# Weight tiles fetched three ahead at 1.25 a slot, k and q loaded as whole rows, and one output tile moved to another PSUM bank, in a linear-attention and two-MLP kernel

## The chip, the cores and the metric

The kernel runs on one core of a Trainium2 chip. The metric is the device time of one execution in microseconds. All times below are microseconds unless marked ns.

## The reference, cut to what matters

Three stages follow each other. The first is a recurrent attention; the other two are MLPs on its output, each with its own nonlinearity. All data are float32.

```python
batch, n_heads, seq, head_dim = (4, 8, 768, 48)
for t in range(S):                                   # attention
    state = alpha[:, :, t, :, None] * state + np.einsum('bhd,bhe->bhde', k[:, :, t], v[:, :, t])
    y[:, :, t] = np.einsum('bhd,bhde->bhe', q[:, :, t], state)
...
x = transpose(y).reshape(3072, 384)
h = x @ w_in                                         # first MLP, w_in 384 x 2048
P = a[0] + a[1] * h + a[2] * h2 + a[3] * h3
Q = 1.0 + np.abs(b[0]) * np.abs(h) + np.abs(b[1]) * h2
x = (P / (Q + 1e-06)) @ w_out                        # w_out 2048 x 384
h = x @ w_in                                         # second MLP
return (h * np.cos(h)) @ w_out
```

The weights come as float64. The kernel reads them as 64-bit words and turns them into float32 on the chip; for the matmuls every float32 operand of the MLPs is then split in a rounded part and the rest, which gives three matmuls for one.

## The kernel before, in words

**Units and slots.** The sequence is cut into 6 chunks of 128 steps; with 4 batches that makes 24 units (`NU`). A unit handles all 8 heads, as 4 pairs: a pair's two heads lie in partitions 0 to 47 and 64 to 111, and the partitions between are padding. A loop over n writes out the program slot by slot. Slot n holds, for different units at once, the stages of a software pipeline: the PE (TensorE) computes `scores(n)`, then `y_state(n - 1)` and `y_scores(n - 1)`, `transposes(n)` and `update0(n - 1)`; ACT (ScalarE) copies and scales (`k_out`, `mask0`, `guess2`, `update2`, `y_out`); DVE (VectorE) computes the decays (`inverse0`, `inverse1`, `guess1`, `decay`, `update1`); POOL (GpSimd) masks and scales k and q (`mask1`, `scale_q`, `scale_k`). Each engine takes its instructions strictly in the written order, so a wait of one instruction holds back all that stand behind it. The program's lines are the order; there is no scheduler.

**Weight tiles.** The first MLP needs 32 weight tiles (16 of `w_in`, 16 of `w_out`), 384 KB each as 64-bit words. `w_fetch` issues the load of the next tile, into one of four places of `spare` (the second x buffer, not yet in use) or of two `raw` buffers; at most six tiles may be begun and not finished (`steps`). `tick(k, ahead)` runs up to k steps of the oldest tile, as long as more than `ahead` tiles are in `steps`. A tile has three steps: the first scales its high words and copies its exponent bytes (L68 on POOL and L69 on ACT while n < 20; L66 and L69, both on ACT, later), the other two are DVE instructions (L73, L74). Then `w_hi` (ACT, L172) rounds the tile and `w_lo` (POOL, L181) forms the rest. While n < 20 the exponent words lie in a PSUM bank (`words_t`, bank b2); from slot 20 on that bank belongs to the MLP and all operands lie in SBUF.

**Loads.** SP (SyncE) issues nearly all DMAs in written order: per slot the unit's a, kq and v, the store of a finished y (`y_store`), and the weight tiles. kq is k and q of a unit, 128 partitions of 4 KB.

**The overlap with the MLPs.** From slot `LEAD` = 20 on, each slot also holds one `layers` step: `gemm1` (9 matmuls of `w_in`, L469), the nonlinearity of earlier tiles (`rational`: ACT, POOL and DVE), and five steps behind, `gemm2` (9 matmuls of `w_out`, L482). Steps after slot 24 hold the MLPs alone. PSUM has eight banks: b0, b1, b2 for `gemm1` (and before that for y, transposes and exponent words), r0 and r1 (r1 holds `fresh`, a constant tile that `decay` and `last_decay` read up to slot 20), and acc0 to acc2 for `gemm2` (and before that for the scores and for the state update u, which lies in acc2).

Of the kernel before, what the change touches and what calls it, by code (L numbers as in the profile page):

```python
# [16 lines left out]
B, H, S, D = 4, 8, 768, 48  # L17
DM, DFF = 384, 2048
NC, C = 6, 128
HP = 4  # L20
# [3 lines left out]
NU = NC * B  # L24
# [14 lines left out]
def attn_then_two_moe(ctx, tc, kqT, aT, vP, w1i, w1o, ma, mb, w2i, w2o, out):  # L39
# [81 lines left out]
    spare = x_p.tile([128, 2, NK, TB], F32R, tag="x", name="spare").rearrange("p a b c -> p (a b c)").bitcast(I32)  # L121
    raw64 = {}
    stage = {}
    slot = [0]
    fetched = [0, 2 * NF]
    steps = []
    to_hi, to_lo = [], []

    def w_fetch(upto):

        i = fetched[0]
        fetched[1] = upto
        if i >= upto or len(steps) > 5 or sum(j >= 28 for j in range(i - len(steps), i + 1)) > 2:
            return
        w = w_order[i]
        fetched[0] += 1
        if i < 28 and i % 6 < 4:
            flat = spare[:, 2 * DM * (i % 6):2 * DM * (i % 6 + 1)]
        else:
            flat = raw_p.tile([128, 2 * DM], I32, tag="raw", name="raw")  # L140
        nc.sync.dma_start(out=flat, in_=(w1i, w1o, w2i, w2o)[2 * w[0] + w[1]][w[2]].bitcast(I32))
        raw64[w] = flat.rearrange("p (a b) -> p a b", b=2)
        steps.append((w, 0))
# [50 lines left out]

    def load(u, name):

        if u >= NU:
            return
        c, b = divmod(u, B)
        ts = {"a": a_t, "kq": kq_t, "v": v_t}[name]  # L200
        t, src = ts[u % len(ts)], {"a": aT, "kq": kqT, "v": vP}[name][c, b]
        if name == "v":
            nc.sync.dma_start(out=t[:, :H * D], in_=src)
        elif u == 0 and name == "a":
            for cs in (slice(0, HP + HP // 2 * C), slice(HP + HP // 2 * C, HP * (C + 1))):
                nc.sync.dma_start(out=t[:, cs], in_=src[:, cs])
        elif u < len(ts):
            nc.sync.dma_start(out=t, in_=src)
        else:
            for j in range(2):  # L210
                js = slice(64 * j, 64 * j + D)
                nc.sync.dma_start(out=t[js], in_=src[js])
        d = U.setdefault(u, {})
        if name == "kq":
            d["k"], d["q"] = t[:, 0], t[:, 1]
        else:
            d[name] = t
# [128 lines left out]
    def y_state(u):  # L346
        c, b = divmod(u, B)
        d = U[u]
        if u >= NU - B:
            d["y"] = ps_acc.tile([128, HP, C], F32, tag="acc2", name="y")  # L350
        else:
            d["y"] = bank("b1", (128, HP, C))
        if c:
            for hp in range(HP):
                nc.tensor.matmul(
                    d["y"][:, hp, :], s_bd[b][:, hp, :], d["q"][:, hp, :], start=hp == 0, stop=False,
                    skip_group_check=True,
                )
# [19 lines left out]
    def y_store(u):  # L378
        c, b = divmod(u, B)
        rows = xd[0][c].rearrange("(a j e) t -> j e a t", a=HP, j=2)  # L380
        for j in range(2):
            nc.sync.dma_start(out=rows[j][:, :, b * C:(b + 1) * C], in_=U[u]["yo"][64 * j:64 * j + D])

    LEAD = NU - 4

    def attention(n, tick):

        def on(u, more=False):
            return 0 <= u < (NU - B if more else NU)
# [50 lines left out]
            transposes(n)  # L440
        if on(n - 1, True):
            update0(n - 1)
        if on(n - 1):
            y_out(n - 1)
        tick(1 if n < LEAD else 2)
        if on(n) and n >= LEAD:
# [214 lines left out]
    with tc.manual_schedule():  # L661
# [16 lines left out]
        for n in range(-3, NU + 1):  # L678
            slot[0] = n
            if n >= -1:  # L680
                load(n + 4, "a")
            if n >= 0:
                if n:
                    load(n + 2, "kq")
                load(n + 1, "v")
                if n >= 2:
                    y_store(n - 2)
                for i in range(min(n, 1) if n < 4 else 2 - n % 2):
                    w_fetch(2 * NF)
            if n == 3:  # L690
                nc.sync.dma_start(out=cab[:, 0:4], in_=ma.unsqueeze(0).to_broadcast([128, 4]))
                nc.sync.dma_start(out=cab[:, 4:6], in_=mb.unsqueeze(0).to_broadcast([128, 2]))
            if n == 6:
                nc.scalar.activation(out=cq[:, 0:2], in_=cab[:, 4:6], func=AF.Abs)
                nc.vector.tensor_scalar(cq[:, 2:6], cab[:, 0:4], -LN_S * LN_S, None, ALU.mult)
            if 8 <= n < 8 + NK:
                x_load(0, 0, n - 8)
            kk = (n - 12) // 2 if n in (12, 14, 16) else None
            if kk is not None:
                x_hi(0, 0, kk)  # L700
            if n == 1:
                warm_up(8)
            attention(n, lambda k: tick(k, 1 if n < LEAD else 1))
            if kk is not None:
                x_lo(0, 0, kk)
            if n == -3:
                for name, u in (("a", 2), ("kq", 1), ("v", 0), ("kq", 2)):
                    load(u, name)
            w_lo([nc.gpsimd])
            if n >= LEAD:  # L710
                layers(n - LEAD)
        y_store(NU - 1)
        for n in range(NU + 1 - LEAD, 2 * N1 + 4):
            layers(n)
# [171 lines left out]
```

## Time and profile before

| what | value |
|---|---|
| time, median of 3 runs | 1007.4 (1005.34 to 1008.27) |
| the profiled execution: time, and its span | 1006.72, 1005.0 |
| busy in the span: PE, DVE, ACT, POOL | 947.7, 667.5, 661.6, 626.5 |
| mean share of TensorE's full clock granted | 0.961 |

The span runs from the first to the last instruction; the profiled time is 1.7 longer. The profiled execution lies 0.7 below the median. Busy times are sums over stages that differ: about the first 190 are attention, the rest the MLPs.

### The profile page before, as it was taken

To read this page: it belongs to the slowest core of one execution; us is meant where nothing else is said; L and a number is where in the kernel's file an instruction comes from. 1 tells how busy PE (TensorE), PEld (TensorE's weight loads), DVE (VectorE), ACT (ScalarE), POOL (GpSimd) and SP (SyncE) were. 2 spreads that over 40 slices of the span, in tenths; PEclk is the share of its full clock that TensorE was granted. 3 is DMA by queue.
4 is the path that set the end of the run, shared out by engine and by line. 5 is a ranking of instruction groups with operands and counts; after the bars stand their busy time and mean duration, and the time that the engine had idled before them with its cause. 6 is when DMAs were issued, how large, how long until landed. Compare 5 with 4: busy or idle time off the path is not lost. (4 is left out here: it accounts for less than half of the span.)

```text
span 1005.0 us, 14055 instructions
## 1 busy us (share of the span) xinstructions
PE 947.7 (94%) x4824; PEld 762.3 (76%) x4824; DVE 667.5 (66%) x1089; ACT 661.6 (66%) x1210; POOL 626.5 (62%) x585
## 2 busy tenths in 40 slices
PE   6688867999999999999999999999999999999997
PEld 5576655787787788888888887688888888888885
DVE  7787866896999999987878985733434334334331
ACT  4776866886888888877778876644445355444442
POOL 4686876997798999997887865533333333333332
PEclk7877787999999999999999999999999999999999
DMA  6888775400332413202015424110010010200001
GB/s 197 235 227 233 206 207 150 117 1 1 100 121 64 149 41 117 72 1 80 1 63 173 126 85 136 32 63 1 1 64 1 0 63 1 64 1 1 32 0 36
DMA packets 46687, 81.91 MB, mean 82 GB/s; under 512 B 5840, under 2 KB 22480, under 8 KB 46608
## 3 DMA queue, kind: packets, MB, share of 16 engines
q1 hardware_dynamic: 46608, 80.93, 27.0%
q8 instruction: 40, 0.66, 0.3%
q14 instruction: 39, 0.32, 0.1%
HBM read 60.47 MB, written 20.45 MB: 81 GB/s over the span
## 5 line engine op out<-in xcount | busy, mean ns | idle before, releaser
L512 POOL TENSOR_TENSOR lo<-g,hi 128x512 fp32r<-128x512 f32 x192 | 256.1, 1334 | 307.0 <-ACT hi L507 300.2
L469 PE MATMUL b<-x,w 128*128 128x512 f32 x1728 | 436.1, 396 | 6.0 <-DVE g L559 3.2
L482 PE MATMUL acc<-hi,w 128*128 128x512 f32 x1152 | 393.4, 396 | 0.1
L469 PEld LDWEIGHTS b<-x,w 128*128 128x128 f32 x1728 | 323.1, 188 | 89.4 <-DVE g L559 7.2
L482 PEld LDWEIGHTS acc<-hi,w 128*128 128x128 f32 x1152 | 216.2, 188 | 54.4 <-ACT o L500 1.3
L507 ACT ACTIVATE hi<-g 128x512 fp32r<-128x512 f32 x192 | 121.4, 633 | 175.9 <-PE acc L482 114.5
L482 PE MATMUL acc<-lo,w 128*128 128x512 f32 x576 | 227.3, 395 | 0.0
L559 DVE TENSOR_TENSOR g<-ah,b 128x512 f32<-128x512 f32 x96 | 65.6, 684 | 133.0 <-ACT ah L557 133.0
L538 POOL TENSOR_TENSOR z<-z,ah 128x512 f32<-128x512 f32 x96 | 126.0, 1312 | 8.0
L482 PEld LDWEIGHTS acc<-lo,w 128*128 128x128 f32 x576 | 108.1, 188 | 25.8
L80 DVE SCALAR_TENSOR_TENSOR ah<-z,b 128x512 f32<-128x512 int32 x96 | 65.7, 684 | 37.6 <-ACT z L79 37.6
L539 DVE TENSOR_TENSOR g<-g,b 128x512 f32<-128x512 f32 x96 | 65.4, 681 | 37.4 <-ACT g L536 36.8
L79 ACT ACTIVATE z<-b 128x512 int32<-128x512 f32 x96 | 57.2, 596 | 49.8 <-PE b L469 49.8
L537 POOL TENSOR_SCALAR z<-ah,cq 128x512 f32<-128x512 f32 x96 | 75.4, 786 | 6.7 <-ACT ah L535 6.5
L536 ACT ACTIVATE g<-b,cq 128x512 f32<-128x512 f32 x96 | 74.5, 776 | 0.0
L543 DVE SCALAR_TENSOR_TENSOR g<-g,cq,r 128x512 f32<-128x512 f32 x96 | 70.9, 738 | 0.1
L530 DVE SCALAR_TENSOR_TENSOR g<-g,cq,b 128x512 f32<-128x512 f32 x96 | 70.8, 737 | 0.0
L535 ACT ACTIVATE ah<-b 128x512 f32<-128x512 f32 x96 | 56.6, 590 | 20.8 <-PE b L469 20.7
L547 ACT ACTIVATE r<-z,lnb 128x512 f32<-128x512 f32 x96 | 66.7, 695 | 3.7 <-DVE tot L604 3.5
L557 ACT ACTIVATE ah<-ah,half_pi 128x512 f32<-128x512 f32 x96 | 68.2, 711 | 0.0
L532 DVE SCALAR_TENSOR_TENSOR r<-z,r 128x512 f32<-128x512 f32 x96 | 65.7, 684 | 0.0
L527 DVE SCALAR_TENSOR_TENSOR z<-z,r 128x512 f32<-128x512 f32 x96 | 65.2, 679 | 0.0
(94 smaller groups left out, 1040.3 us busy)
## 6 DMA issues: line engine op xcount, KB each, us to landing
kq<-kqT SPq DMA_DIRECT2D x40, 192.0 KB, 4.9
raw<-w2i SPq DMA_DIRECT2D x16, 384.0 KB, 3.1
raw<-w2o SPq DMA_DIRECT2D x16, 384.0 KB, 3.1
w<-wd SPq DMA_DIRECT2D x16, 384.0 KB, 3.2
v<-vP SPq DMA_DIRECT2D x24, 192.0 KB, 3.6
spare<-w1i SPq DMA_DIRECT2D x12, 384.0 KB, 4.1
x<-x0d SPq DMA_DIRECT2D x18, 256.0 KB, 3.3
x1d<-o SPq DMA_DIRECT2D x18, 256.0 KB, 2.3
```

What stands on the lines that cost most here:

```text
L80: nc.vector.scalar_tensor_tensor(r, k, -TWO_PI, h, ALU.mult, ALU.add)
L469: nc.tensor.matmul(h, ws[0][f][:, w, ks], x[:, xx, kk, :], start=i == 0, stop=i == 8)
L482: nc.tensor.matmul(acc[k], ws[1][f][:, w, ks], d[g], start=f == 0 and i == 0, stop=f == NF - 1 and i == 2)
L507: nc.scalar.activation(out=t["hi"], in_=t["g"], func=AF.Copy)
L512: eng.tensor_tensor(out=t["lo"], in0=t["g"], in1=t["hi"].bitcast(F32), op=ALU.subtract)
L530: nc.vector.scalar_tensor_tensor(g, g, cq[:, 3:4], two["h"], ALU.add, ALU.mult)
L536: nc.scalar.activation(out=g, in_=h, func=AF.Identity, scale=cq[:, 5:6], bias=cq[:, 4:5])
L537: nc.gpsimd.tensor_scalar(zz, ah, cq[:, 1:2], cq[:, 0:1], ALU.mult, ALU.add)
L538: nc.gpsimd.tensor_tensor(out=zz, in0=zz, in1=ah, op=ALU.mult)
L543: nc.vector.scalar_tensor_tensor(g, g, cq[:, 2:3], r, ALU.add, ALU.mult)
L547: nc.scalar.activation(out=r, in_=two["z"], func=AF.Ln, scale=LN_S, bias=lnb)
L557: nc.scalar.activation(out=two["r"], in_=two["r"], func=AF.Sin, bias=half_pi)
```

## The change

The change does four things. A tile is converted only when more than three tiles are begun (`tick(k, 3 ...)` in place of 1, for n < 20), and tiles are fetched one a slot and two in each fourth slot, starting at slot 0, in place of one and two in turn from slot 4 on. Since `spare` holds tiles up to number 23 (before: 27) and the two `raw` buffers all later ones, the condition that limits tiles in `raw` is written with the same function. kq is always loaded by one DMA of 128 rows, in place of two of 48 rows. The y of unit 20 goes to bank r1 in place of acc2, and from slot 20 on `y_out` stands behind `layers`.

```diff
+    LEAD = NU - 4
...
+    def in_spare(i):
+        return i < 24 and i % 6 < 4
+
     def w_fetch(upto):
...
-        if i >= upto or len(steps) > 5 or sum(j >= 28 for j in range(i - len(steps), i + 1)) > 2:
+        if i >= upto or len(steps) > 5 or sum(not in_spare(j) for j in range(i - len(steps), i + 1)) > 2:
             return
...
-        if i < 28 and i % 6 < 4:
+        if in_spare(i):
...
-        elif u < len(ts):
+        elif u < len(ts) or name == "kq":
             nc.sync.dma_start(out=t, in_=src)
...
-        if u >= NU - B:
+        if u > LEAD:
             d["y"] = ps_acc.tile([128, HP, C], F32, tag="acc2", name="y")
+        elif u == LEAD:
+            d["y"] = bank("r1", (128, HP, C))
         else:
             d["y"] = bank("b1", (128, HP, C))
...
-        if on(n - 1):
+        if on(n - 1) and n < LEAD:
             y_out(n - 1)
...
-                for i in range(min(n, 1) if n < 4 else 2 - n % 2):
+                for i in range(min(n, 1) if n % 4 else 2):
                     w_fetch(2 * NF)
...
-            attention(n, lambda k: tick(k, 1 if n < LEAD else 1))
+            attention(n, lambda k: tick(k, 3 if n < LEAD else 1))
...
             if n >= LEAD:
                 layers(n - LEAD)
+                y_out(n - 1)
```

**SP, slots 0 to 2** (`spare<-w1i` is a weight tile's load, `kq<-kqT` the load of k and q, `x0d<-g` a store of y). Before:

```order
L203 DMA v_107<-vP 128x384
L212 DMA a_101<-aT 48x516 x2
L208 DMA kq_105<-kqT 128x1024
L203 DMA v_108<-vP 128x384
L141 DMA spare<-w1i 128x768
L212 DMA a_100<-aT 48x516 x2
L212 DMA kq_102<-kqT 48x1024 x2
L203 DMA v_106<-vP 128x384
L382 DMA x0d<-g 48x4x128 x2
L141 DMA spare<-w1i 128x768
```

and with the change:

```order
L208 DMA v_107<-vP 128x384
L145 DMA spare<-w1i 128x768 x2
L217 DMA a_101<-aT 48x516 x2
L213 DMA kq_105<-kqT 128x1024
L208 DMA v_108<-vP 128x384
L145 DMA spare<-w1i 128x768
L217 DMA a_100<-aT 48x516 x2
L213 DMA kq_102<-kqT 128x1024
L208 DMA v_106<-vP 128x384
L389 DMA x0d<-g 48x4x128 x2
L145 DMA spare<-w1i 128x768
```

The first two tiles now stand ahead of slot 1's loads, the third and fourth where the first and second stood, and kq is one row in place of two. In both programs the first conversion step stands in slot 2.

**ACT, slot 21** (`yo` is the copy of unit 20's y, `ah` and the `g` behind it read the first tile of `gemm1`, `sc` is the scores, the `w` rows are `w_hi`). Before:

```order
L66 ACTIVATE st<-raw 128x384
L69 ACTIVATE raw<-raw 128x384
L297 ACTIVATE hi<-sc_1967 128x512
L297 ACTIVATE lo<-sc_1968 128x512
L257 ACTIVATE r_1983<-r_1983 128x512
L258 ACTIVATE r_1983,chk<-r_1983 128x512
L342 ACTIVATE s_bd_144<-s_c_148 48x4x48 x2
L376 ACTIVATE yo<-y 128x512
L535 ACTIVATE ah<-b_1946 128x512
L536 ACTIVATE g<-b_1946,cq 128x512
```

and with the change:

```order
L66 ACTIVATE st<-raw 128x384
L69 ACTIVATE raw<-raw 128x384
L302 ACTIVATE hi<-sc_1906 128x512
L302 ACTIVATE lo<-sc_1907 128x512
L262 ACTIVATE r_1922<-r_1922 128x512
L263 ACTIVATE r_1922,chk<-r_1922 128x512
L347 ACTIVATE s_bd_144<-s_c_148 48x4x48 x2
L540 ACTIVATE ah<-b_1884 128x512
L541 ACTIVATE g<-b_1884,cq 128x512
L176 ACTIVATE w_9_134<-st 128x384
L383 ACTIVATE yo<-r_1939 128x512
```

The copy of y has moved behind the first two instructions of the nonlinearity and reads bank r1.

**DVE, MLP steps 5 and 6** (the first two steps after slot 24; L73 and L74, in the changed file too, are a weight tile's second and third step, the rest the nonlinearity). Before, from the `z` row of step 5 on:

```order
L527 SCALAR_TENSOR_TENSOR z<-z,r_2223 128x512
L530 SCALAR_TENSOR_TENSOR g<-g,cq,b_2152 128x512
L532 SCALAR_TENSOR_TENSOR r_2223<-z,r_2223 128x512
L539 TENSOR_TENSOR g<-g,b_2197 128x512
L543 SCALAR_TENSOR_TENSOR g<-g,cq,r_2223 128x512
L527 SCALAR_TENSOR_TENSOR z<-z,r_2256 128x512
L530 SCALAR_TENSOR_TENSOR g<-g,cq,b_2197 128x512
L532 SCALAR_TENSOR_TENSOR r_2256<-z,r_2256 128x512
```

and with the change:

```order
L532 SCALAR_TENSOR_TENSOR z<-z,r_2162 128x512
L535 SCALAR_TENSOR_TENSOR g<-g,cq,b_2085 128x512
L537 SCALAR_TENSOR_TENSOR r_2162<-z,r_2162 128x512
L544 TENSOR_TENSOR g<-g,b_2136 128x512
L548 SCALAR_TENSOR_TENSOR g<-g,cq,r_2162 128x512
L74 SCALAR_TENSOR_TENSOR st<-raw,st 128x384
L532 SCALAR_TENSOR_TENSOR z<-z,r_2203 128x512
L535 SCALAR_TENSOR_TENSOR g<-g,cq,b_2136 128x512
L537 SCALAR_TENSOR_TENSOR r_2203<-z,r_2203 128x512
L544 TENSOR_TENSOR g<-g,b_2177 128x512
L548 SCALAR_TENSOR_TENSOR g<-g,cq,r_2203 128x512
L73 SCALAR_TENSOR_TENSOR st<-st,raw 128x384
```

Before, all 32 tiles are finished in slot 24; with the change four and a part of a fifth are left for MLP steps 5 to 11. Counted over the whole program, 26 tiles were converted with their exponent words in PSUM and 6 with all operands in SBUF; now 21 and 11. In slots 4 to 19 the L73 rows fall from 24 to 19, and the tiles fetched from 24 to 19.

## Rows read from the trace of the kernel before

**Rows 1.** Windows: each stretch's length, busy us by engine, granted clock, DMA share, GB/s

```profile
34.10:155.70 121.60, 95.82 (x954) 80.59 (x952) 90.89 (x213) 87.35 (x197) 95.21 (x113) 0.78 0.82 219
155.70:180.40 24.70, 17.47 (x158) 14.20 (x155) 14.14 (x27) 15.75 (x35) 16.01 (x16) 0.86 0.47 130
...
195.70:1005.00 809.30, 798.13 (x3405) 637.14 (x3403) 523.02 (x769) 526.76 (x913) 481.27 (x408) 1.00 0.16 53
...
195.70:250.00 54.30, 54.30 (x234) 43.75 (x233) 44.82 (x74) 42.99 (x73) 47.71 (x43) 1.00 0.04 15
```

**Rows 2.** Groups by line, 34.1 to 155.7: busy, mean ns, idle before, releasers

```profile
L181 POOL TENSOR_TENSOR w<-st,w 128x384 fp32r<-128x384 f32 x23 | 24.1, 1058 | 0.0
...
L73 DVE SCALAR_TENSOR_TENSOR b<-st,b 128x384 int32<-128x384 int32 x24 | 13.5, 562 | 22.3 <-POOL st L68 18.3 <-ACT b L69 3.9
...
L74 DVE SCALAR_TENSOR_TENSOR st<-spare,b 128x384 int32<-128x384 int32 x16 | 8.7, 545 | 0.0
L68 POOL TENSOR_SCALAR st<-spare 128x384 f32<-128x384 f32 x16 | 8.5, 533 | 26.2 <-DMA spare<-w1i 19.3 <-DMA spare<-w1o 6.9
...
L69 ACT ACTIVATE b<-spare 128x384 int32<-128x384 uint8 x16 | 8.3, 519 | 29.3 <-DMA spare<-w1i 16.7 <-DMA spare<-w1o 6.5 <-DVE st L74 5.9
```

**Rows 3.** Timeline of ACT, slots 12 to 14: start, us, instruction, idle before

```profile
100.55 0.58 ACT L297 ACTIVATE hi<-sc 128x512 f32<-128x512 f32 x1
...
105.96 0.58 ACT L297 ACTIVATE hi<-sc 128x512 f32<-128x512 f32 x1
...
115.41 0.51 ACT L69 ACTIVATE b<-spare 128x384 int32<-128x384 uint8 x1 [3.55 <-DMA spare<-w1i]
115.86 0.58 ACT L297 ACTIVATE hi<-sc 128x512 f32<-128x512 f32 x1
```

**Rows 4.** Timeline of PE: start of slot 4, then slots 13 and 14

```profile
34.06 1.16 PE L290 MATMUL sc<-kq 48*128 48x128 f32 x16
...
104.12 2.08 PE L355 MATMUL b<-kq,s_bd 128*128 128x128 f32 x8 [1.30 <-ACT g L376]
...
110.10 1.26 PE L290 MATMUL sc<-kq 48*128 48x128 f32 x16
111.29 1.16 PE L355 MATMUL b<-kq,s_bd 128*128 128x128 f32 x8
...
114.08 0.67 PE L322 MATMUL u<-v,g 128*64 128x48 f32 x16
```

**Rows 5.** Timeline, slots 20 to 22, PE and ACT

```profile
155.72 1.16 PE L290 MATMUL sc<-kq 48*128 48x128 f32 x16
...
161.43 0.55 ACT L66 ACTIVATE st<-spare 128x384 f32<-128x384 f32 x1 [3.23 <-DMA spare<-w1o]
...
170.78 2.04 PE L355 MATMUL y<-kq,s_bd 128*128 128x128 f32 x8 [6.19 <-DVE s_c L336]
...
174.66 2.60 PE L469 MATMUL b<-x,w 128*128 128x512 f32 x9
...
180.40 2.36 PE L469 MATMUL b<-x,w 128*128 128x512 f32 x9
```

**Rows 6.** DMA, 34.1 to 155.7: GB/s in 40 slices; issues, KB, us to landing

```profile
GB/s 172 276 327 181 215 156 194 322 277 258 190 227 242 184 289 192 344 219 109 249 221 266 217 144 235 160 246 236 122 269 188 281 202 133 247 228 301 145 74 235
...
kq<-kqT SPq DMA_DIRECT2D x34, 192.0 KB, 4.9
spare<-w1i SPq DMA_DIRECT2D x9, 384.0 KB, 3.9
```

**Rows 7.** The page's DMA issues: the first units' kq, whole rows

```profile
kq<-kqT SPq DMA_DIRECT2D x4, 512.0 KB, 4.1
```

**Rows 8.** Groups by line, 300 to 400: weight steps with all operands in SBUF

```profile
L74 DVE SCALAR_TENSOR_TENSOR st<-raw,st 128x384 int32<-128x384 int32 x10 | 12.6, 1264 | 0.1
...
L73 DVE SCALAR_TENSOR_TENSOR st<-st,raw 128x384 int32<-128x384 int32 x10 | 7.8, 783 | 0.4 <-ACT raw L69 0.2
```

**Rows 9.** Timeline of PE at MLP step 5

```profile
193.53 2.37 PE L469 MATMUL b<-x,w 128*128 128x512 f32 x9 [1.07 <-DVE g L530]
```

More of the change, by code (lines that the diff above doesn't have):

```diff
@@ L382, in y_store @@
             nc.sync.dma_start(out=rows[j][:, :, b * C:(b + 1) * C], in_=U[u]["yo"][64 * j:64 * j + D])
-    LEAD = NU - 4
     def attention(n, tick):
```

## Prediction

> **What bounds the kernel now.** I first cut the span into stages, by windows [rows 1]. From 195.7 to the end, 809.3, PE is busy 798.1 at the full granted clock: a step of 18 large matmuls takes 809.3 / 192 = 4.2, and nothing but fewer PE waits can shorten this part. So the kernel's time is the moment at which PE becomes saturated, plus about 809. What the change touches lies ahead of that. In the stretch 34.1 to 155.7, slots 4 to 19 (121.6, or 7.6 a slot), no engine is saturated: PE 95.8, POOL 95.2, DVE 90.9, ACT 87.4 busy.
>
> Why they idle there is shown by the groups by line [rows 2]. The weight tile's first step waits for its load: POOL sat idle 26.2 ahead of L68, ACT 23.2 (16.7 + 6.5) ahead of L69, both until a DMA landed, and DVE 18.3 ahead of L73 for POOL. These are the same waits seen from three engines, not a sum. The timeline of ACT shows the pattern [rows 3]: from the score copy of slot 12 to that of slot 13 is 105.96 - 100.55 = 5.4, and to the next 9.9, of which 3.55 is ACT standing before L69 for a tile that was issued in the same slot. Everything behind it in ACT's order, the score copies first, is held too.
>
> The second place is slots 20 and 21 [rows 5]. From the scores of unit 20 (155.72) to the third MLP tile (180.40) go 24.7, in which PE is busy 17.5 [rows 1]. PE waits 6.19 at the first matmul of unit 20's y, because that y shares bank acc2 with the state update, and in the slot before ACT waits 3.23 for a weight tile.
>
> **The change part by part.**
>
> *Tiles three ahead, 1.25 a slot (slots 4 to 19).* A tile loaded two slots before its use has some 12 us to land; loads take 3.9 [rows 6]. I take the DMA waits of L68 and L69 as gone. Also five of 24 conversions leave the stretch: POOL loses 5 x (0.533 + 1.058) = 8.0, DVE 5 x (0.562 + 0.545) = 5.5 [rows 2]. What is then late next is an engine. Lower bound by work: POOL 95.2 - 8.0 = 87.2, DVE 85.4, PE at the full clock 16 x 4.65 = 74.4 (a slot at that level runs from 110.10 to 114.08 + 0.67 [rows 4]). So 87 / 16 = 5.5 a slot is the floor. The two slots of [rows 3] without their DMA wait take 5.4 and 6.35; they hold four and five conversion steps, and the changed order has 57 such steps in 16 slots, 3.6 each. Upper bound: nothing gained, 7.6. I take 6.2, nearer to the two slots without waits than to today's mean but above the floor, since four engines that wait for each other don't reach 100%: 16 x 6.2 = 99, **-22.4**. That is less than POOL's 26.2 of waits.
>
> *kq as whole rows.* In 16 slots it adds 16 x (512 - 2 x 192) = 2048 KB and the five tiles fewer take away 5 x 384 = 1920 KB, so the stretch still moves about 0.219 x 121.6 = 26.6 MB, plus 0.1. One issue of SP in each slot goes, which nobody waits for here. The first four kq, whole, landed in 4.1 after issue, the halves in 4.9 [rows 6, 7], so I cost it at **0**; its cover is the slot between load and use. DMA's own limit: 0.82 of its time is busy [rows 1], 99.7 of 121.6. If packets stayed as slow, 100 would be the floor of the stretch, just my 99; single slices reach 327 and 344 GB/s [rows 6], at which 26.7 MB take about 80. The floor lies between the two, and I take it as not binding. The Trainium skill ("DMA: Bandwidth & Descriptors", Specifications) puts HBM's limit for one core at about 358 GB/s; by that figure, an estimate, the stretch would need 75 and DMA would never bind. The trace's best slice stays below it, and no stretch here holds such a rate.
>
> *Unit 20's y in r1, y copied later (slots 20, 21).* With r1 free since slot 20 the wait of 6.19 falls away, and the tiles converted there were fetched slots before, so ACT's 3.23 too. Behind them PE still needs its own work: 17.47 busy at 0.86 of the clock is 15.0 at full clock, so the gain is at most 24.7 - 15.0 = 9.7. It is at least some 3, if only the DMA wait goes and y then waits for the masks on POOL. I take **-7**: the two waits make 9.4, less what POOL (16.0 busy) takes of it. The later copy of y stands behind two to four ACT instructions of the MLP; PE needs its bank again a slot later, which covers it at no cost; uncovered, it keeps the gain of these slots at its lower end of 3.
>
> *Four and a half conversions moved into MLP steps 5 to 11.* In their new place L73 and L74 take 0.78 + 1.26 = 2.05 [rows 8]. DVE without conversions is busy 44.82 of 54.3 [rows 1], 0.825. Seven steps: 29.4 available, 24.3 + 4.7 x 2.05 = 33.9 wanted, 4.5 too much. Banks ahead of PE may hide some of it, but at step 5 PE already waits 1.07 for DVE [rows 9], so little is stored up. From 0 to +4.5; I take **+3**.
>
> Sum: against the profiled 1006.7, -22.4 - 7 + 3 = -26.4 gives 980.3. The median of the runs is 0.7 higher, so 981.
>
> **The rivals.**
>
> *A second limit just behind the first.* Slots of 6.9, either because DMA packets stay slow (0.82 x 121.6 = 99.7 at 90% is 111) or because PE keeps the mixed clock: it is granted 0.78 on average in the stretch, and at the lower of its two levels (1.2 GHz) the eight matmuls of y's state part take 2.08, at the upper (2.4 GHz) 1.16 [rows 4]; 95.8 of PE work and 13% of idle time make 110. For it: both numbers are of today. Against it: slices of 327 and more; and PE's idle time, 25.8 in this stretch, is what the change shortens. -11.2 - 7 + 3 makes 992. The Trainium skill ("TensorE: Matmul & The Clock Gate", Part 1) says that the throttled level is the default and activity releases it; by that rule PE's share of this rival falls away and the stretch is bounded by 74.4 of PE work. The trace agrees as far as it goes: 1.00 is granted where PE is busy 798.1 of 809.3 [rows 1].
>
> *The full gain.* The slots reach 5.7, just above POOL's floor: 121.6 - 91 = -30.4, with -8 and +1: 970. For it: the two slots in [rows 3]. Against it: DMA at 0.82 of its time already.
>
> *The change doesn't do what it says.* The load is one of several waits that end together; without it POOL and ACT wait for DVE or PE as long. ACT has such a wait (5.9 for L74 [rows 2]). Then the slots keep 7.5 or so, and with a smaller gain at unit 20 (-3) and +3 the time is about 1006.
>
> *Slower: whole rows choke the DMA queue.* All loads share SP's queue; if whole kq rows lower the rate at which it can be served, kq and a arrive late, and each slot waits for POOL's `scale_q`. It decides at 121.6 + 7 - 3 = 125.6 for the stretch: 26.7 MB in that time is 213 GB/s, below today's 219. At 200 GB/s it is 134, +12.4, and the time about 1016. For it: a third more bytes of kq. Against it: four whole loads that land sooner than halves, and slices far above the rate.
>
> **How the numbers follow.** Forecast (974 to 989) 0.52; second limit 0.22; full gain 0.16; no effect 0.05; slower 0.05. The likeliest case gives 981. The range 968 to 999 leaves out the far end of the full gain (slots at 5.5 and -9.7 would be about 964), the slow tail of the second limit, no effect and slower: about 0.18. A difference of 0.3% (3 us) is what runs of this kernel can tell from none; the first three cases lie beyond it, so faster 0.90, same 0.05, slower 0.05.
>
> **What would show it.** Right: idle ahead of L68 and L69 for `spare` and `raw` nearly gone; 34.1 to 155.7's counterpart, from unit 4's to unit 20's scores, near 99; granted clock there above 0.85; from unit 20's scores to the third MLP tile about 18, with no wait at y's first matmul; a few us of PE waits for DVE in steps 5 to 12, absent before. Wrong: new idle time ahead of `scale_q` or `decay` for kq or a (DMA), scores at the lower clock without waits (PE), or a stretch after unit 20 that gives back more than 5.

## The result, and the profile after

The changed kernel takes 978.71 (median of 4 runs, 977.98 to 979.64) against 1007.2 for the kernel before (4 runs): a ratio of 0.9719, with a 95% interval of 0.9698 to 0.974. The forecast was 981, with a range of 968 to 999. The profiled execution of the changed kernel is one of 979.64 with a span of 977.9, so it lies 0.9 above the median, where that of before (1006.72) lay 0.5 below the 1007.2; the spans differ by 27.1, the medians by 28.5.

The change adds lines, so what was L290, L322, L355, L376, L469, L530 is now L295, L327, L362, L383, L474, L535; L66 to L80 stay.

Windows of the changed kernel, cut where [rows 1] were cut (unit 4's scores, unit 20's scores, third MLP tile, end), with one more from the third to the twenty-first MLP tile; columns as there:

```profile
33.80:129.80 96.00, 77.75 (x956) 64.99 (x952) 84.34 (x201) 82.90 (x189) 89.25 (x104) 0.93 0.90 277
129.80:146.70 16.90, 14.93 (x159) 12.20 (x155) 13.54 (x29) 15.62 (x36) 14.75 (x16) 1.00 0.57 172
...
146.70:977.90 831.20, 814.15 (x3506) 647.25 (x3504) 550.18 (x796) 545.14 (x953) 503.87 (x428) 1.00 0.17 56
...
146.70:227.80 81.10, 76.97 (x366) 59.90 (x365) 78.35 (x113) 65.84 (x120) 73.41 (x65) 1.00 0.20 61
```

Slots 4 to 19 take 96.0 in place of 121.6, at 0.93 of the clock in place of 0.78, and DMA moves 277 GB/s in place of 219. POOL is busy 89.25 of the 96.0 and is now the nearest limit. Slots 20 and 21 take 16.9 in place of 24.7. From there to the end 831.2 are needed, where before it was 1005.0 - 180.4 = 824.6. The three differences, -25.6, -7.8 and +6.6, with 0.3 less ahead of unit 4, make the 27.1. The last of these is the surprise. The page's line of the clock in 40 slices shows the same in short: but for the first, all lie at 0.8 or more.

```profile
PEclk7988999999999999999999999999999999999999
```

The groups by line of 33.8 to 129.8, against [rows 2]:

```profile
L185 POOL TENSOR_TENSOR w<-st,w 128x384 fp32r<-128x384 f32 x20 | 19.9, 1003 | 0.0
L73 DVE SCALAR_TENSOR_TENSOR b<-st,b 128x384 int32<-128x384 int32 x19 | 10.6, 559 | 3.7 <-POOL st L68 2.1 <-ACT b L69 1.4
L68 POOL TENSOR_SCALAR st<-spare 128x384 f32<-128x384 f32 x13 | 6.9, 540 | 0.0
L69 ACT ACTIVATE b<-spare 128x384 int32<-128x384 uint8 x13 | 6.7, 518 | 7.9 <-DVE st L74 7.9
L68 POOL TENSOR_SCALAR st<-raw 128x384 f32<-128x384 f32 x6 | 3.3, 552 | 0.0
```

The 26.2 of POOL's idle time ahead of L68 are gone entirely, and ACT's 23.2 of waits for DMA ahead of L69 too. What is left there is the wait of ACT for L74, 7.9 for `spare` and 2.2 for `raw`, as large as before (9.4 for both in that stretch). The chain of waits of the same stretch (engine, line, awaited; us, times, longest) names what comes behind:

```profile
ACT b L69 <- DVE st L74: 10.1, 8, 2.7
...
PE u L327 <- DVE pc L248: 7.7, 6, 1.7
...
POOL kq L287 <- DMA kq<-kqT: 1.0, 2, 0.8
```

The first two are waits of compute engines for each other. A wait for a load is left, of POOL's `scale_k` (L287) for kq: 0.20 and 0.84.

The timeline of slots 20 to 22, against [rows 5]:

```profile
129.84 1.16 PE L295 MATMUL sc<-kq 48*128 48x128 f32 x16
...
131.09 0.56 ACT L66 ACTIVATE st<-spare 128x384 f32<-128x384 f32 x1
...
135.09 0.67 PE L327 MATMUL u<-v,g 128*64 128x48 f32 x16 [1.97 <-DVE pc L248]
...
139.07 1.16 PE L362 MATMUL r<-kq,s_bd 128*128 128x128 f32 x8
...
146.68 2.37 PE L474 MATMUL b<-x,w 128*128 128x512 f32 x9
```

Unit 20's y (now out<-in `r<-kq,s_bd`) starts without the 6.19 of idle time, and L66 without its 3.23. PE's largest remaining wait is 1.97 for the decays of DVE.

### The profile page after: what moved, and what is told of

Read it like the earlier page. It is cut to its first block, busy times and chain, and to the rows that moved or that the text cites. A ratio compares the mean times of both kernels' runs of the same rounds, so it can differ in the third digit from the quotient of the medians.

```text
span 977.9 us, 13991 instructions
## 1 busy us (share of the span) xinstructions
PE 929.0 (95%) x4824; PEld 743.6 (76%) x4824; DVE 675.0 (69%) x1089; ACT 661.7 (68%) x1215; POOL 627.0 (64%) x580
## 5 line engine op out<-in xcount | busy, mean ns | idle before, releaser
L474 PE MATMUL b<-x,w 128*128 128x512 f32 x1728 | 436.7, 396 | 9.1 <-DVE g L535 6.2
L474 PEld LDWEIGHTS b<-x,w 128*128 128x128 f32 x1728 | 322.0, 188 | 95.0 <-DVE g L535 10.6
L80 DVE SCALAR_TENSOR_TENSOR ah<-z,b 128x512 f32<-128x512 int32 x96 | 65.6, 683 | 37.7 <-ACT z L79 37.7
L79 ACT ACTIVATE z<-b 128x512 int32<-128x512 f32 x96 | 57.0, 593 | 50.0 <-PE b L474 50.0
L535 DVE SCALAR_TENSOR_TENSOR g<-g,cq,b 128x512 f32<-128x512 f32 x96 | 70.8, 737 | 0.0
L540 ACT ACTIVATE ah<-b 128x512 f32<-128x512 f32 x96 | 56.4, 587 | 15.3 <-PE b L474 15.0
```

The costliest lines, as they stand in the source:

```text
L474: nc.tensor.matmul(h, ws[0][f][:, w, ks], x[:, xx, kk, :], start=i == 0, stop=i == 8)
L535: nc.vector.scalar_tensor_tensor(g, g, cq[:, 3:4], two["h"], ALU.add, ALU.mult)
```

## The experiments

Twelve kernels ran, each cut from the kernel before or the changed one by one or two edits. The table gives for each the median, its ratio to the kernel before, run beside it, with the 95% interval, and the length of the stages in its profile, read from the starts of PE's rows: slots 4 to 19, slots 20 and 21, third to twenty-first MLP tile, from there to the sixty-first, and the rest.

| kernel | median | ratio | slots 4-19 | 20-21 | tiles 3-21 | 21-61 | rest |
|---|---|---|---|---|---|---|---|
| before | 1007.2 | 1 | 121.7 | 24.7 | 76.6 | 171.1 | 576.8 |
| changed | 978.71 | 0.9719 (0.9698 to 0.974) | 96.0 | 16.8 | 81.1 | 172.3 | 577.9 |
| before + y part | 1002.17 | 0.995 (0.9929 to 0.9971) | 120.8 | 19.7 | 77.1 | 171.0 | 576.6 |
| before + whole kq | 1011.59 | 1.0046 (1.0024 to 1.0068) | 124.1 | 24.7 | 76.6 | 171.1 | 577.9 |
| before + three ahead | 987.17 | 0.9806 (0.9765 to 0.9847) | 103.5 | 22.9 | 77.6 | 172.3 | 576.5 |
| before + 1.25 a slot | 993.21 | 0.9857 (0.9817 to 0.9897) | 109.2 | 17.9 | 78.6 | 171.2 | 578.1 |
| before + both | 982.63 | 0.9739 (0.9705 to 0.9773) | 95.9 | 20.6 | 80.9 | 171.4 | 576.7 |
| changed, kq in halves | 978.4 | 0.972 (0.9698 to 0.9743) | 95.3 | 16.9 | 81.1 | 171.0 | 576.5 |
| changed, late DVE steps short | 976.39 | 0.9704 (0.9681 to 0.9728) | 95.7 | 16.9 | 78.3 | 171.1 | 578.0 |
| changed, no late DVE steps | 975.42 | 0.9677 (0.9641 to 0.9713) | 95.5 | 16.6 | 78.0 | 171.1 | 577.9 |
| changed, late steps spread | 978.12 | 0.9718 (0.9695 to 0.974) | 95.2 | 16.4 | 80.0 | 171.0 | 578.0 |
| changed, drained early, spread | 980.27 | 0.9738 (0.9713 to 0.9764) | 99.9 | 15.3 | 79.5 | 171.0 | 578.3 |
| changed, halves and spread | 976.15 | 0.9671 (0.9646 to 0.9696) | 96.8 | 18.4 | 79.7 | 172.2 | 576.6 |
| changed, one tile a slot | 981.65 | 0.9731 (0.9698 to 0.9763) | 86.4 | 15.9 | 91.5 | 171.2 | 578.3 |

The kernel before had medians of 1006.7 to 1009.6 in the sets in which these ran, so medians of different sets compare only to some 3; there the ratios decide.

The last two columns take one of two values each, 171.0 to 171.4 or 172.2 to 172.3 and 576.5 to 576.8 or 577.9 to 578.3, in kernels whose instructions there are the same. The first differs at one place, between the 54th and the 55th tile: in the changed kernel L73 takes 1.68 there (at 370.21) and PE then waits 0.86 for DVE, with halves the same L73 takes 0.55 (at 369.04) and PE doesn't wait. The second differs behind the last tile, where 18.9 to 19.0 or 20.3 to 20.8 follow its first matmul. That second value stands in all seven profiles with whole kq rows and in one of the seven with halves; whether kq's form has a part in it, one profile for each kernel can't tell. I don't count a difference of 1 to 3 behind tile 21 as the effect of an edit.

**The y part alone.** The kernel before with these edits:

```diff
...
-        if u >= NU - B:
+        if u > LEAD:
             d["y"] = ps_acc.tile([128, HP, C], F32, tag="acc2", name="y")
+        elif u == LEAD:
+            d["y"] = bank("r1", (128, HP, C))
...
-        if on(n - 1):
+        if on(n - 1) and n < LEAD:
             y_out(n - 1)
...
                 layers(n - LEAD)
+                y_out(n - 1)
```

> The kernel before with the y part alone (unit 20's y in r1, y copied behind the MLP step). Theory: the wait of 6.2 at y's first matmul goes, ACT's wait for a weight tile in slot 20 stays, so 5 to 7 us less: 1000 to 1002. Rival (the y part only works together with the tiles fetched early, since ACT's wait holds unit 20's scores copy anyway): within 2 us of before.

Slots 20 and 21 fell by 5.0 and the median by 5, as expected. The timeline of the same slots shows both halves of the expectation: ACT's wait for the tile stays, y's matmuls no longer wait.

```profile
160.63 0.55 ACT L66 ACTIVATE st<-spare 128x384 f32<-128x384 f32 x1 [3.27 <-DMA spare<-w1o]
...
163.71 1.16 PE L358 MATMUL r<-kq,s_bd 128*128 128x128 f32 x8
...
170.73 1.23 PE L291 MATMUL sc<-kq 48*128 48x128 f32 x16 [2.47 <-POOL kq L278]
```

Of the 6.19 that y waited, 5.0 arrive in the stage. A new wait of PE for POOL's `scale_q` (2.47) has taken a part.

**Whole kq rows alone.**

```diff
-        elif u < len(ts):
+        elif u < len(ts) or name == "kq":
             nc.sync.dma_start(out=t, in_=src)
```

> The kernel before with kq loaded as whole rows alone. Theory: the loads are hidden, 0 within 2 us of 1007. Rival 1 (halves crowd the DMA queue, so whole rows let weight tiles land sooner and shorten the waits at L68 and L69): 4 to 8 us less. Rival 2 (a third more bytes delay the weight tiles): 3 to 6 us more.

It is slower by 0.46%, some 4 to 5 us (its interval is clear of 1), as the second rival had it. Yet DMA is not choked. Its window and waits:

```profile
33.50:157.60 124.10, 94.37 (x956) 78.79 (x952) 90.99 (x213) 87.43 (x199) 95.49 (x114) 0.79 0.77 232
```

```profile
POOL st L68 <- DMA spare<-w1i: 19.2, 5, 4.9
...
PE sc L290 <- POOL st L68: 12.9, 5, 2.9
...
POOL st L68 <- DMA spare<-w1o: 8.8, 3, 4.3
```

232 GB/s were moved at a busy share of 0.77, where the halves need 0.82 for 219 [rows 1]: 95.6 of DMA time for 28.85 MB against 99.7 for 26.67 MB. Whole rows cost DMA less time although they carry more. The loss is elsewhere. POOL's wait for the tile, already on the path, grew from 26.2 to 28.1, and PE's wait for scores behind POOL's L68 from 9.9 to 12.9. With one tile on its way the tile's load stands in SP's queue behind the longer kq, and its moment of landing is what the slot waits for. The loads bear this out in part: of the eight tiles that POOL waits for in this stretch, the last seven took 4.6 on average from issue to landing against 4.1 before, the first 4.0 against 6.6; over all 24 tiles the mean is the same, 4.6. The Trainium skill ("DMA: Bandwidth & Descriptors", Rules for kernel authors) advises one transfer over 128 partitions in place of two on disjoint halves. By the DMA time that agrees here, by the time of this kernel it does not, as long as a tile is awaited behind it. My 0 for this part missed the case in which it stands alone.

**kq in halves again, in the changed kernel**, the reverse test:

```diff
-        elif u < len(ts) or name == "kq":
+        elif u < len(ts):
             nc.sync.dma_start(out=t, in_=src)
```

> The changed kernel with kq loaded as two halves again. kq alone made the kernel before slower (ratio 1.0046), since the longer load stands ahead of the weight tiles that were waited for. Theory (the price of kq is paid only through the weight tile's wait, which three tiles ahead remove): within 2 us of the changed kernel, ratio 0.970 to 0.974. Rival 1 (kq's price is fixed): 4 us faster, ratio 0.967. Rival 2 (in shorter slots DMA limits and whole rows are the cheaper form: 235 GB/s at 0.79 busy against 224 at 0.83): 3 to 6 us slower, ratio 0.975 to 0.978.

978.4, the same as the changed kernel within 0.3. Halves are 0.94 busy at 259 GB/s and whole rows 0.90 at 277 in the window of slots 4 to 19, and little waits for either: POOL 0.7 for halves, 1.0 for whole rows. The two runs together say that the cost of kq's longer rows is paid through the awaited tile. With tiles ahead it is 0, as forecast.

```profile
34.20:129.50 95.30, 77.87 (x956) 65.21 (x952) 84.33 (x201) 82.85 (x189) 89.29 (x103) 0.93 0.94 259
```

**Three tiles ahead alone**, at the old rate:

```diff
-            attention(n, lambda k: tick(k, 1 if n < LEAD else 1))
+            attention(n, lambda k: tick(k, 3 if n < LEAD else 1))
```

> The kernel before with three tiles ahead alone, fetched at the old 1.5 a slot. By the program's order 24 tiles are converted before slot 20 (before: 26) and the other eight in slots 20 to 24. Theory (the DMA wait is the loss): the waits at L68 and L69 go, the stretch from unit 4's to unit 20's scores falls from 121.6 to about 102, of which slots 20 to 24 give back some 5 because eight conversions crowd there: about 992. Rival (the loss is the number of conversions a slot, not the wait): the stretch stays above 115, the time above 1002.

It gives 987.17, that is 20 less, and slots 4 to 19 take 103.5. The window, and the groups by line of 33 to 160:

```profile
32.70:136.10 103.40, 82.36 (x954) 69.04 (x952) 88.79 (x211) 86.26 (x195) 94.44 (x111) 0.90 0.95 260
```

```profile
L68 POOL TENSOR_SCALAR st<-spare 128x384 f32<-128x384 f32 x16 | 8.5, 542 | 0.0
L69 ACT ACTIVATE b<-spare 128x384 int32<-128x384 uint8 x16 | 8.4, 522 | 8.2 <-DVE st L74 8.1
```

All DMA waits of the tiles are gone, but 24 conversions remain, and POOL is busy 94.4 of 103.4: the earlier load alone brings 18 of the 25.7 us of this stage. The time lies 5 below the expected 992: of the 5 that slots 20 to 24 were to give back, slots 20 and 21 gave none (22.9 against 24.7) and tiles 3 to 21 gave 1.0. With a DMA share of 0.95 a wait for another load has come, of POOL's `scale_q` for kq:

```profile
POOL kq L282 <- DMA kq<-kqT: 4.0, 3, 1.8
```

**1.25 tiles a slot alone**, one ahead as before:

```diff
-        if i >= upto or len(steps) > 5 or sum(j >= 28 for j in range(i - len(steps), i + 1)) > 2:
+        if i >= upto or len(steps) > 5 or sum(not (j < 24 and j % 6 < 4) for j in range(i - len(steps), i + 1)) > 2:
...
-        if i < 28 and i % 6 < 4:
+        if i < 24 and i % 6 < 4:
...
-                for i in range(min(n, 1) if n < 4 else 2 - n % 2):
+                for i in range(min(n, 1) if n % 4 else 2):
```

> The kernel before with the new rate of 1.25 a slot alone, conversion still one tile ahead. By the program's order tiles are mostly converted a slot after their fetch, in each fourth slot in the same slot as the fetch; 24 are converted before slot 20, about three fall into MLP steps 5 to 8. Theory: about four of the eight DMA waits of 3 to 4 us remain, the stretch falls to about 108, +2 in the MLP steps: about 996. Rival (the wait needs three tiles ahead): stretch above 115, time above 1002. Rival (rate is all): stretch below 100.

993.21, that is 14 less, with 109.2 in the stage. The waits for the load remain, fewer of them and now partly for `raw`:

```profile
L68 POOL TENSOR_SCALAR st<-spare 128x384 f32<-128x384 f32 x13 | 7.0, 539 | 8.5 <-DMA spare<-w1i 5.5 <-DMA spare<-w1o 3.0
...
L68 POOL TENSOR_SCALAR st<-raw 128x384 f32<-128x384 f32 x8 | 4.2, 529 | 8.7 <-DMA raw<-w1o 6.0 <-DMA raw<-w1i 2.7
```

8.5 + 8.7 = 17.2 of POOL's waiting is left of 26.2. In an early slot, at 17.2, POOL waits 6.28 for the first tile, and unit 4's scores start 4.5 later than before; three ahead would not have asked for that tile yet.

**Both together**, without the kq and y parts: the last two diffs in one kernel.

> The kernel before with the two weight edits together (three tiles on their way and 1.25 a slot), k and q still in halves, unit 20's y as before. If both edits remove the same DMA waits, their effects overlap: alone they gave 20 and 14 us, together I expect 23 to 26 less than before, a median of 981 to 984, and a stretch of slots 4 to 19 of 95 to 97 with no DMA wait ahead of L68 and L69. What is missing to the changed kernel's 28.5 is then the part of unit 20's y. Rival: whole rows of k and q were needed for the stretch to become short; then it stays near 100 or above here, with idle time ahead of L282 or L287 for kq, and the median at 986 or more.

982.63, a median in the expected range, though the 27.0 to the kernel before beside it (1009.6) are 1 more than expected. Slots 4 to 19 take 95.9, within 0.1 of the changed kernel, and the rival falls: POOL waits for a kq in halves once, for 1.7. So the two edits overlap: alone -20 and -14, together -25.8 in this stage, -4.1 in slots 20 and 21 and +4.3 in tiles 3 to 21. The whole of the changed kernel's gain in slots 4 to 19 is theirs. The y part then accounts for 20.6 - 16.8 = 3.8 in slots 20 and 21; alone it was 5.0, since 4.1 of what the changed kernel saves there come from the tiles. In the ratios, 0.9739 and 0.9719, these 3.8 don't show clear of the intervals.

**One tile a slot.** The changed kernel with

```diff
-                for i in range(min(n, 1) if n % 4 else 2):
+                for i in range(min(n, 1)):
```

> The changed kernel with one weight tile fetched per slot instead of 1.25: by the order of its instructions 16 conversions instead of 19 to 20 in slots 4 to 19, two more in slots 20 to 24 and three more in MLP steps 5 to 15. Theory: POOL, busy 89 of 96, now bounds the stretch. Three to four conversions at 0.54 + 1.00 of POOL's time are 4.6 to 6, so the stretch comes to 90 to 92; slots 20 and 21 lose 1 to 2, and three more late conversions cost about 1 us each behind the third MLP tile: 978 to 979 in all, with the time moved from one stage to the other. Rival: the stretch is held by the chain of PE, ACT and DVE, not by POOL's work; then it stays at 95 to 97, and the time is 982 to 985.

The stage fell by 9.6, to 86.4 where I expected 90 to 92, and by more than POOL's work (89.25 to 83.13, 6.1 less); it is 0.96 busy now, so POOL is the limit of this stage and the rival of a chain of PE, ACT and DVE falls. But tiles 3 to 21 went from 81.1 to 91.5, +10.4, where I had expected about 3.

```profile
32.40:118.90 86.50, 73.37 (x958) 62.38 (x954) 82.52 (x197) 80.51 (x182) 83.13 (x96) 0.96 0.93 295
...
134.80:226.30 91.50, 80.11 (x366) 62.32 (x365) 87.60 (x122) 71.98 (x134) 81.19 (x71) 0.96 0.21 65
```

Two places make most of it:

```profile
139.98 1.82 PE L295 MATMUL sc<-kq 48*128 48x128 f32 x16 [2.83 <-POOL kq L282]
...
211.61 3.91 PE L474 MATMUL b<-x,w 128*128 128x512 f32 x9 [3.68 <-DVE g L535]
```

Between the third and the fourth tile 4.2 are lost, where PE waits 2.83 for POOL's `scale_q` and then runs at the lower clock (the scores take 1.82 in place of 1.16). Of the 6.2 behind that, 4.8 lie around the 18th tile, where PE waits 3.68 for DVE and its nine matmuls then take 3.91 in place of 2.37. DVE is busy 87.60 of the 91.5. The same work thus has one price in slots 4 to 19, through POOL, and another behind slot 20, through DVE and at one place through POOL; and at 1.25 a slot the two are about in balance. The ratios, 0.9731 here and 0.9719 for the changed kernel, don't differ clear of noise; the median lies between my 978 to 979 and the rival's 982 to 985.

**The late DVE steps on 32 of 384 columns.** In MLP steps 5 to 15 of the changed kernel the two DVE steps of a tile work on 32 columns, so those tiles are converted in part only (`cut` takes the first 32 columns in these steps):

```diff
...
-            lambda: nc.vector.scalar_tensor_tensor(both, ti, 3, low, ...),
-            lambda: nc.vector.scalar_tensor_tensor(ti, hi, -0x80000000, both, ...),
+            lambda: nc.vector.scalar_tensor_tensor(cut(both), cut(ti), 3, cut(low), ...),
+            lambda: nc.vector.scalar_tensor_tensor(cut(ti), cut(hi), -0x80000000, cut(both), ...),
```

> The changed kernel; the two DVE steps of the weight tiles that fall into MLP steps 5 to 15 work on 32 of 384 columns, so those tiles are converted in part only. From the third MLP tile to the end the changed kernel takes 831.2, before 824.6. Theory (DVE work of the moved tiles makes these 6.6): about 825 to 826 there, PE waits for DVE in MLP steps 3 to 20 under 2, time about 973. Rival (the later copy of y, or ACT's and POOL's share of those tiles): 829 or more, time above 976.5.

Tiles 3 to 21 take 78.3 in place of 81.1, so 2.8 of the stage's 4.5 are the price of these steps' columns. From the third tile to the end it is 827.3, and the median 976.39: between the theory (825 to 826; 973) and the rival (829; 976.5). The groups by line of 146 to 230 (L79 and L80 are L73 and L74 of the changed kernel) are odd:

```profile
L80 DVE SCALAR_TENSOR_TENSOR st<-raw,st 128x32 int32<-128x32 int32 x5 | 4.6, 929 | 0.1
L79 DVE SCALAR_TENSOR_TENSOR st<-st,raw 128x32 int32<-128x32 int32 x4 | 2.1, 528 | 0.1
```

A twelfth of the columns still takes 929 ns. DVE's and POOL's timelines side by side tell why:

```profile
165.49 1.30 DVE L80 SCALAR_TENSOR_TENSOR st<-raw,st 128x32 int32<-128x32 int32 x1
166.72 0.67 DVE L538 SCALAR_TENSOR_TENSOR z<-z,r 128x512 f32<-128x512 f32 x1
...
177.60 0.18 DVE L80 SCALAR_TENSOR_TENSOR st<-raw,st 128x32 int32<-128x32 int32 x1
```

```profile
165.45 1.30 POOL L549 TENSOR_TENSOR z<-z,ah 128x512 f32<-128x512 f32 x1
166.70 1.29 POOL L523 TENSOR_TENSOR lo<-g,hi 128x512 fp32r<-128x512 f32 x1
...
177.59 1.36 POOL L549 TENSOR_TENSOR z<-z,ah 128x512 f32<-128x512 f32 x1
```

The short step that starts 0.04 behind a POOL instruction ends with it and takes 1.30. Eight of the nine short steps end 0.04 to 0.05 behind the end of a POOL instruction, whatever their length (0.23 to 1.30). The ninth starts at 177.60, within 0.01 of a POOL instruction, and takes 0.18; that POOL instruction takes 1.36 in place of 1.30. But for it, the duration of such a step is what is left of the POOL instruction beside it. The Trainium skill ("SBUF — State Buffer", SBUF: two separate sides) says that a DVE instruction with two SBUF inputs and a GpSimd instruction share one port pair, which the one that starts first holds for its whole length. The eight steps agree, and of the ninth the starts lie too close to tell.

**No late DVE steps at all.** Tiles that begin in MLP steps 5 to 15 leave out both steps, and their first step writes zeros:

```diff
...
-            lambda: nc.vector.scalar_tensor_tensor(both, ti, 3, low, ...),
-            lambda: nc.vector.scalar_tensor_tensor(ti, hi, -0x80000000, both, ...),
+            lambda: None if skip else nc.vector.scalar_tensor_tensor(both, ti, 3, low, ...),
+            lambda: None if skip else nc.vector.scalar_tensor_tensor(ti, hi, -0x80000000, both, ...),
```

> The changed kernel without the two DVE steps of the four tiles that begin in MLP steps 5 to 15 (these tiles are set to zero by their first step, so their conversion is left out). With the same steps cut to 32 columns, third to twenty-first MLP tile fell only from 81.1 to 78.3 of the 76.6 before the change, and the short steps still took up to 1.3 us, each until the POOL instruction beside it ended. Theory: the price of a late step is the POOL instruction that it has to wait out, not its columns; without the eight steps the stage comes to 76.5 to 77.3 and PE waits for DVE g there for at most 1.5. Rival: what is left is the ACT and POOL share of these tiles (first step, rounding, rest); then the stage stays at 78 or above.

78.0, hardly less than with short steps, and just in the rival's range. So once DVE has some of its time back, a short step that waits out a POOL instruction costs PE nearly nothing. My theory set the price at that wait; by these runs it goes with the sum of DVE's work (busy 78.35, 74.77 with short steps, 71.96 without), and only as long as that sum binds. What remains of the stage, 78.0 - 76.6 = 1.4, isn't explained by these steps. PE still waits in two places, 1.5 in all, as the theory allowed:

```profile
159.85 2.36 PE L480 MATMUL b<-x,w 128*128 128x512 f32 x9 [0.84 <-DVE g L541]
211.16 2.37 PE L480 MATMUL b<-x,w 128*128 128x512 f32 x9 [0.64 <-DVE g L541]
```

By the starts of the tiles, 0.5 of the 1.4 lies between the third and the seventh tile, and the y part alone has the same 0.5 there (77.1), without any late conversion. The other 0.9 lies at the 18th tile, behind the wait of 0.64. Ahead of it DVE's own work on x and the checks, 8 instructions (L599, L605 to L609) with operands in SBUF, takes 7.9, where it took 3.3 before: one of 128x48 takes 1.24 in place of 0.19, and POOL, which had a pause of some 0.6 in each step there before, runs almost without one. So the same collision goes on for instructions that the change didn't touch, probably because POOL has the late tiles' `w_lo` to do as well; no run took those away, so this is argued, not shown.

**The late steps spread**, two and one in turn:

```diff
-            tick(0 if n < 4 else 2)
+            tick(0 if n < 4 else 2 - n % 2)
```

> The changed kernel with three weight-tile steps in two MLP steps in place of four, from step 4 to 15, so that the moved tiles end two steps later. Theory (DVE is over its 4.2 a step only because the tiles come too densely): 3.47 of other work + 0.5 x 2.05 = 4.5 a step in place of 4.85 leaves half of the overload: 2 to 3 us faster than the changed kernel, ratio about 0.969. Rival (the work has to be done before steps 11 to 13 add x's split, so its sum decides, not its density): within 1 us.

1.1 less in tiles 3 to 21, nothing in the median that could be measured (978.12): the rival. How densely DVE's work stands matters less than its sum.

**Drained early, and spread.** With the last diff, and the tiles in waiting worked off from slot 18 on:

```diff
-            attention(n, lambda k: tick(k, 3 if n < LEAD else 1))
+            attention(n, lambda k: tick(k, 3 if n < LEAD - 2 else 1))
```

> As the run with the moved tiles spread, and from slot 18 on tiles are converted when more than one is begun (before slot 18 still three), so that 22 or 23 in place of 21 are done with their exponent words in PSUM. Theory (DVE pays 1.1 for a tile there and 2.05 later, and slot 19 has no conversion step at all): slots 18 to 20 lose 2, the steps after gain 3 to 4: 1 to 2 us faster than the spread run. Rival (slots 18 and 19 are bound by DVE too, and a wait for the tiles fetched last comes back): as fast as the spread run or up to 3 us slower.

Against the changed kernel slots 4 to 19 lose 3.9, slots 20 and 21 gain 1.5, tiles 3 to 21 gain 1.6; the median, 980.27, is 1.6 above the changed kernel and 2.2 above the spread one, where 1 to 2 less were expected. The rival has the time right but not all of its reason: no wait for a weight tile comes back. POOL is busy 92.60 in the first stage, so DVE work moved from late to early is paid there, the mirror image of one tile a slot.

**Halves and spread together.** Both single diffs in the changed kernel.

> The changed kernel with k and q in two halves again and with the late weight steps spread, 2 and 1 in turn instead of 2 in each MLP step. Alone each was within 1 us of the changed kernel. If each is worth the 0.3 to 0.6 us that its median showed, 977 to 978; if both differences were only noise, 978 to 979.5. A time below 976 would say that late steps and k and q loads collide, which neither run alone has shown.

976.15, 2.6 below the changed kernel's median and below the expected 977 to 978, though not under the 976 that would have spoken for a collision. The interval of its ratio (0.9646 to 0.9696) ends just below the start of the changed kernel's (0.9698), in a set in which the kernel before took 1009.6. Its profiled execution was its slowest of six (979.12), so its stages show no gain, and I can't name where one would come from. Setting aside the two with work left out, it is by its ratio the fastest version; its gain over the changed kernel was not measured beside it.

## Why the prediction was right, and where it was off

The time came within 2.3 of the forecast, and on the forecast's mechanism. That it came so near has some luck in it: by the profiles the forecast was 4.3 too cautious about the gains (-3.2, -0.8 and the 0.3 ahead of unit 4) and 3.6 too cheap behind the third MLP tile, and these errors offset each other. The terms of the sum were these.

*Slots 4 to 19: -25.6, forecast -22.4.* The step was right: idle time ahead of L68 and L69 went from 26.2 and 23.2 to nothing. The stage came to 6.0 a slot, where I took 6.2, with a floor by POOL's work of 5.5 (87; it is busy 89.25, since `w_lo` went from 23 to 20 in the stretch and not by five). The earlier load alone (103.5) and the lower rate alone (109.2) show that neither edit would have done it by itself, both together (95.9) that no other part was needed.

*Whole kq rows: 0, forecast 0.* Right for the change as it stands, by kq in halves. As a property of the edit it was wrong: alone it costs 0.46%, some 4 to 5. The cover that I named, the slot between kq's own load and its use, holds but for the 1.0 that POOL waits for kq. I had not asked what stands behind kq in SP's queue.

*Slots 20 and 21: -7.8, forecast -7.* Right, and both waits went as described. The copy of y behind `layers` shows as a wait of PE of 0.18 at one place (155.01).

*The late conversions: forecast +3, from 0 to +4.5.* This is the part of the sum that was furthest off. Behind the third MLP tile the profile lost 6.6, but some 2 of it (172.3 - 171.1 and 577.9 - 576.8) lie behind tile 21: with halves and the same late conversions these columns read 171.0 and 576.5. So the prediction's own sign of being wrong, more than 5 given back after unit 20, appears in this one profile (6.6) and not with halves (4.0). What the stage itself lost is 81.1 - 76.6 = 4.5, the upper bound of the estimate. DVE is busy 78.35 of 81.1, where before it was 63.45 of 76.6:

```profile
180.40:257.00 76.60, 75.53 (x365) 60.41 (x364) 63.45 (x103) 60.55 (x105) 64.45 (x60) 1.00 0.14 39
```

PE's rows show little reserve: five waits for `guess1` in place of the one of [rows 9].

```profile
160.30 2.37 PE L474 MATMUL b<-x,w 128*128 128x512 f32 x9 [0.82 <-DVE g L535]
...
173.68 2.36 PE L474 MATMUL b<-x,w 128*128 128x512 f32 x9 [0.52 <-DVE g L535]
187.07 2.37 PE L474 MATMUL b<-x,w 128*128 128x512 f32 x9 [0.54 <-DVE g L535]
197.17 2.36 PE L474 MATMUL b<-x,w 128*128 128x512 f32 x9 [1.43 <-DVE g L535]
214.66 2.37 PE L474 MATMUL b<-x,w 128*128 128x512 f32 x9 [0.42 <-DVE g L535]
```

They sum to 3.73 against 1.07. Yet the late steps themselves cost about what the term said: leaving out the two DVE steps of four tiles takes 3.1 of the 4.5 away. The other 1.4 (0.5 between the third and the seventh tile, 0.9 at the 18th) stays without them and has no place in the sum, which priced only the moved steps. So neither the discount of 1.5 for banks ahead of PE nor its absence is shown; the mis-sized part is what else the stage lost. The single steps were priced well enough: 1.37 for L74 and 0.86 for L73 in 146.7 to 230, 2.23 for both, against 2.05 from [rows 8].

```profile
L74 DVE SCALAR_TENSOR_TENSOR st<-raw,st 128x384 int32<-128x384 int32 x9 | 12.3, 1370 | 0.2
...
L73 DVE SCALAR_TENSOR_TENSOR st<-st,raw 128x384 int32<-128x384 int32 x9 | 7.7, 860 | 2.9 <-ACT raw L69 1.6 <-POOL lo L307 1.3
```

*The rivals.* The second limit did not bind: DMA rose to 277 GB/s, and the granted clock to 0.93. But it wasn't far: DMA is 0.90 busy here and 0.94 with halves, and 0.95 with three ahead alone, where POOL waits 4.0 for kq. The best slice of the stretch, one fortieth of it, is 394 GB/s, above the 344 of before and above the limit that the prediction set beside that. The clock fell to its lower level (1.2 GHz) only twice between 44.5 and 129.8, as the windows show, which I cut where the level changes:

```profile
44.50:65.40 20.90, 15.33 (x196) 12.65 (x195) 16.49 (x40) 17.51 (x43) 19.00 (x23) 1.00 0.91 278
65.50:72.20 6.70, 6.16 (x46) 5.18 (x48) 6.55 (x15) 6.18 (x14) 5.75 (x8) 0.50 0.97 299
72.30:89.30 17.00, 14.44 (x195) 12.24 (x196) 14.05 (x35) 13.63 (x31) 15.16 (x19) 1.00 0.97 298
89.40:96.10 6.70, 5.61 (x36) 4.43 (x35) 6.26 (x16) 6.17 (x16) 6.55 (x8) 0.50 0.66 216
96.20:129.80 33.60, 27.73 (x376) 23.37 (x374) 30.90 (x73) 30.39 (x70) 31.97 (x37) 1.00 0.88 266
```

The prediction cited from the Trainium skill ("TensorE: Matmul & The Clock Gate", Part 1) that activity releases the throttle. The traces agree: with fewer waits the granted clock rose from 0.78 to 0.93, and PE's work shrank from 95.8 to 77.75 of busy time for the same instructions (x954, x956). This part of the gain shows in no engine's waits; how much of the 25.6 it makes was not measured by itself. "It doesn't do what it says" is excluded by L68's idle time of 0.0. The queue choked by whole rows did not happen in that way, since DMA's busy share fell; that whole rows can make the kernel slower was true all the same, in the kernel before.

## What to carry to other kernels

Here a longer load cost nothing by itself, but some 4 where an awaited load stood behind it in its queue: price an edit of one transfer by the next transfer's waiter. Edits that remove the same wait don't add: here 20 and 14 made 25 to 27, and a look at the order tells beforehand that both feed the same wait. Work that is moved out of a stage has a price where it goes; when the engine there is near its limit, price the stage and not only the moved steps: here these cost 3.1 and the stage lost 4.5, and the next tiles moved cost more than the first.

## What the runs showed of the hardware

DVE's steps with two SBUF operands (L73, L74) took from 0.18 to 1.30 on the same 128x32; eight of nine ended 0.04 to 0.05 behind a POOL instruction that was in progress, like the one at 165.49 behind that of 165.45. Other DVE instructions on SBUF data do the same: a check of 128x48 took 0.19 in a pause of POOL (at 236.65 of the kernel before) and 1.24 where it began 0.10 behind a POOL instruction (207.64, without late steps), ending 0.04 behind it. One DMA of 128 rows of kq, 512 KB, landed in 4.9 like one of 48 rows with 192 KB [rows 6], and the stretch with whole rows moved 277 GB/s at 0.90 of DMA's time, with halves 259 at 0.94.

```profile
kq<-kqT SPq DMA_DIRECT2D x17, 512.0 KB, 4.9
```
